# Column-tiled dense products ahead of weighting passes, and a reordered prologue, in a fused attention and gated-MLP kernel

## The chip, the cores and the metric

One core of a Trainium2 chip runs the whole program. The time is device microseconds of one execution. Before the change it is 325.08 us, the median of three runs (324.86 to 325.14). The profile is one further execution of the same program.

In a profile, PE is the matrix engine (TensorE) and PEld its weight loads, DVE is VectorE, ACT ScalarE, POOL GpSimd, SP the engine that issues the DMAs here. A product is one TensorE instruction: a stationary tile (the weights, up to 128 rows by 128 columns) against a moving tile whose columns (up to 512) stream through.

## What is computed

```python
xn = layernorm(x)                              # 2048 rows, 640 columns
q, k, v = xn @ wq, xn @ wk, xn @ wv            # 32 heads of 20 columns, 4 segments of 512 rows
for s in range(4):
    p = softmax(qs @ ks.T * 20**-0.5 + causal mask)      # within the segment
    a_dot = p @ vs
    a_mem = (phi(qs) @ M) / (phi(qs) @ z + 1e-6)         # memory of the segments before
    o = g * a_mem + (1 - g) * a_dot                      # g = sigmoid(beta), per head
    M, z = M + phi(ks).T @ vs, z + sum(phi(ks))          # phi(t) = t + 1 if t > 0 else exp(t)
s = o @ wo
h = (sigmoid(xn @ w_gate) * (xn @ w_up)) @ w_down        # 1536 hidden columns
out = x + s * silu(h)
```

Inputs and output are bf16.

## The kernel before, in words

**Tiling.** The rows are worked in four segments of 512 rows, four tiles of 128 rows each. The 640 columns are five chunks of 128 (DC = 5), and two halves of 320 (HB) where an output has rows on the partitions. Nearly all of the matrix work consists of dense products with a full 128x128 stationary tile and a moving tile of 512 columns (k_chunk, q_chunk, gate, up: lines 322, 354, 463, 475) or of 320 columns (v_tile, down, o_proj: lines 396, 488, 534), accumulated over the chunks in one of four PSUM buffers (dtile). Two smaller ones update and read the memory (m_update, mem_read: lines 422, 442).

**Attention.** Eight groups of four heads are worked in four pairs per segment. The scores of a pair are computed in five units (UNITS, line 42), one unit per slot: a unit issues 8 or 16 products whose stationary tiles have 24 rows, four side by side in the array's row strips (scores, line 556), and ACT then takes the exponential of the whole unit (line 567). A weighting pass (weigh_group, line 605) multiplies the exponentials of one group with V: 28 products in seven rounds of four, each with a 128x32 stationary tile, the four of a round side by side in the array's column strips (line 613). It runs at the start of slot u = 3 for the pair's first group, and at the start of the next pair's slot u = 0 for its second. The very last pair is weighted in another way (weigh, line 578). One further set of products uses column strips, q_bound (line 369), once per segment.

**The order of the work** is written out: all five engines run their instructions in the order in which the program issues them. A planner (lines 718 to 848) goes through 20 slots per segment, 80 in all. Tasks have due times in slots (PLAN, line 61), and the tasks of segment n + 1 (LayerNorm, V, K, Q, phi) and of segment n - 1 (output projection) fall among the slots of segment n. The products of the gated MLP are the filling (bulk): each slot gets a share such that dense work per slot is level, with less where a weighting pass follows (TURN, line 55). In a slot, the order is: weighting pass if there is one, scores, dense work. LAG (line 57) sets how long after a pass its output is transposed by a DMA (LAG[0]) and divided (LAG[1], LAG[2]).

**The prologue** is startup (line 651), with the loads from line 188 on ahead of it. SP issues rows 0, 1 and 2 of x (x_first, 128 rows each), the left half of Wv, rows 3, the right half of Wv, Wk, Wq and the rest. PE first runs 40 dummy products on the identity (warm, line 646). For each 128 rows DVE takes the statistics (ln_stats, line 267), POOL the reciprocal root, DVE normalizes (ln_norm, line 288), PE transposes in five products (line 300), and ACT copies the transposed rows out of PSUM into xnT (line 301). Then come the V products of rows 0 to 2, the five chunks of K and of Q, and the first chunks of the MLP. POOL also fills what has to be constant: the three key tiles KT with ones (lines 653, 671, 674; 128 x 2048 bf16 each), the columns of ones in the V tiles (v_ones), the head indicators (make_ind) and the block diagonal (make_bd).

Of the kernel before, what the change touches and what calls it, by code (L numbers as in the profile page):

```python
# [56 lines left out]
LAG = [0.8, 2.9, 1.7]  # L57
# [4 lines left out]
    dict(glu=[0.3, -0.46],  # L62
         v=[0.1, 0.64, 1.13, 2.21, 2.84, 3.31, 3.7, 5.69],
         k=[6.2, 6.62, 7.76, 8.11, 9.34],
         q=[9.4, 10.58, 11.42, 11.93, 15.22],
         pk=[9.1, 9.21, 10.27, 11.45, 12.74],
         pq=[14.8, 15.82, 16.1, 17.26, 18.26],
         pk0=[-1.0, -0.69, 1.1, 1.4, 2.04],
         bound=16.1,
         upd=[5.8, 9.09],  # L70
         norm=[-2.2, 0.23],
         late=4.2),
    dict(v=[2.5, 3.15, 4.01, 4.25, 4.7, 4.98, 5.8, 6.15],
         k=[6.2, 6.89, 7.97, 8.13, 8.97],
         q=[12.6, 13.11, 13.88, 14.24, 15.01],
         pk=[10.2, 10.65, 10.99, 12.53, 13.51],
         pq=[14.9, 14.96, 16.25, 16.53, 18.03],
         bound=16.5,
         upd=[9.4, 10.15],
         stats=[-2.0, -0.87, -1.23, 0.15],  # L80
         norm=[0.6, 0.88, 1.63, 3.19],
         proj=[5.7, 6.67, 7.51, 8.45, 9.23, 9.75, 10.77, 11.29],
         read=[2.4, 3.01, 3.92, 4.48, 4.72, 5.2, 6.11, 6.62]),
    dict(v=[3.2, 3.6, 4.46, 4.9, 5.46, 6.06, 6.33, 6.88],
         k=[7.6, 8.55, 9.39, 11.57, 12.48],
         q=[12.8, 13.01, 13.89, 14.4, 14.62],
         pq=[14.5, 16.3, 16.56, 17.42, 18.23],
         bound=15.8,
         upd=[9.7, 12.3],
         stats=[-1.9, -1.66, -0.06, 1.16],  # L90
         norm=[-0.4, 0.1, 1.3, 2.5],
         proj=[4.0, 5.18, 5.84, 6.61, 7.43, 8.68, 9.21, 9.37],
         read=[3.1, 3.6, 5.1, 5.4, 6.8, 7.2, 8.1, 8.6]),
    dict(proj=[5.9, 6.42, 7.54, 8.41, 9.04, 9.62, 10.89, 12.0],
         read=[2.0, 3.79, 4.35, 5.57, 5.85, 7.03, 7.64, 8.63]),
# [4 lines left out]
def kernel(  # L100
# [65 lines left out]


# [15 lines left out]
    def load_proj(name, src, c0=0, c1=D):  # L183
        if c0 == 0:
            W[name] = cpool.tile([P, DC, D], BF, name=f"W{name}")
        nc.sync.dma_start(W[name][:, :, c0:c1], src[:, c0:c1].rearrange("(c p) n -> p c n", p=P))
# [29 lines left out]
    nhalf = cpool.tile([P, 2], F32, name="nhalf")  # L216
# [14 lines left out]
    def v_ones(a, b):  # L231
        for i in range(a, b):
            nc.gpsimd.memset(V[i][:, :, DH:VW], 1.0)
            nc.gpsimd.memset(V[i][:, H, 0:DH], 1.0)
# [32 lines left out]
    def ln_stats(n, p, i0=0, i1=2):  # L267
        s = st[n]
        x = s[f"x{p}"]
        if i0 == 0:  # L270
            s[f"mv{p}"] = lnp.tile([P, 2, 2], F32, name="mv")
            s[f"rstd{p}"] = lnp.tile([P, 2], F32, name="rstd")
        mv, rstd = s[f"mv{p}"], s[f"rstd{p}"]
        for i in range(i0, i1):
            bs = lnp.tile([P, 2, 6], F32, name="bs")
            nc.vector.bn_stats(bs[:, 0, :], x[:, i, 0:HB])
            nc.vector.bn_stats(bs[:, 1, :], x[:, i, HB:D])
            nc.vector.bn_aggr(mv[:, i, :], bs[:])

        def root():  # L280
            nc.gpsimd.tensor_scalar(rstd[:, i0:i1], mv[:, i0:i1, 1], EPS, None, op0=ALU.add)
            nc.gpsimd.tensor_tensor(rstd[:, i0:i1], rstd[:, i0:i1], nhalf[:, i0:i1], op=ALU.pow)
        if n <= 1:
            root()
        else:
            later(0.6, root)

    def ln_norm(n, p, i):
        s = st[n]
        if "xnT" not in s:  # L290
            s["xnT"] = xpool.tile([P, DC, L], BF, name="xnT")
        xn = lnp.tile([P, D], BF, name="xn")
        nc.vector.tensor_scalar(xn[:], s[f"x{p}"][:, i, :], s[f"mv{p}"][:, i, 0:1], s[f"rstd{p}"][:, i:i + 1],  # L293
                                op0=ALU.subtract, op1=ALU.mult)
        j = 2 * p + i
        dst = s["xnT"][:, :, j * P:(j + 1) * P]
        if n == 0:
            pT = dtile([P, DC, P], BF, "pT")
            for c in range(DC):
                nc.tensor.transpose(pT[:, c, :], xn[:, c * P:(c + 1) * P], ident[:])  # L300
            nc.scalar.copy(dst, pT[:])
# [20 lines left out]
    def k_chunk(n, c):  # L322
        s = st[n]
        if c == 0:
            s["k5"] = stg.tile([P, DC, L], BF, name="k5")
            s["kabs"] = stg.tile([P, DC], F32, name="kabs")
        ps = dtile([P, L], F32, "psk")
        for k in range(DC):
            nc.tensor.matmul(ps[:], lhsT=W["k"][:, k, c * P:(c + 1) * P], rhs=s["xnT"][:, k, :],  # L329
                             start=(k == 0), stop=(k == DC - 1))  # L330
# [23 lines left out]
    def q_chunk(n, c):  # L354
# [5 lines left out]
        for k in range(DC):  # L360
            nc.tensor.matmul(ps[:], lhsT=W["q"][:, k, c * P:(c + 1) * P], rhs=s["xnT"][:, k, :],  # L361
                             start=(k == 0), stop=(k == DC - 1))
# [33 lines left out]
    def v_tile(n, j, half):  # L396
        s = st[n]
        ps = dtile([P, HB], F32, "psv")
        for k in range(DC):
            nc.tensor.matmul(ps[:], lhsT=s["xnT"][:, k, j * P:(j + 1) * P],  # L400
                             rhs=W["v"][:, k, half * HB:(half + 1) * HB],
                             start=(k == 0), stop=(k == DC - 1))
        va = V[4 * (n % 2) + j]
        evacuate(va[:, half * 16:(half + 1) * 16, 0:DH], ps[:].rearrange("p (h e) -> p h e", e=DH))
# [17 lines left out]
    def m_update(n, cs):  # L422
        s = st[n]
        dm = dtile([P, len(cs), HW * VW], F32, "dm")
        for i, c in enumerate(cs):
            w = (H1[c] - H0[c]) * VW
            for j in range(4):
                nc.tensor.matmul(dm[:, i, 0:w], lhsT=s["pkt"][:, j, c * P:(c + 1) * P],  # L428
                                 rhs=V[4 * (n % 2) + j][:, H0[c]:H1[c], :].rearrange("p h e -> p (h e)"),
                                 start=(j == 0), stop=(j == 3))  # L430
# [11 lines left out]
    def mem_read(n, j, b):  # L442
# [5 lines left out]
        for i, c in enumerate(parts):  # L448
            lo, hi = max(H0[c], 16 * b), min(H1[c], 16 * b + 16)
            nc.tensor.matmul(am[:, lo - 16 * b:hi - 16 * b, :].rearrange("p h e -> p (h e)"),  # L450
                             lhsT=s["q5"][:, c, j * P:(j + 1) * P],
                             rhs=Mbd[:, c, lo - H0[c]:hi - H0[c], :].rearrange("p h e -> p (h e)"),
                             start=(i == 0), stop=True, skip_group_check=True)
# [9 lines left out]
    def gate(n, f):  # L463
# [3 lines left out]
        for k in range(DC):  # L467
            nc.tensor.matmul(gp[:], lhsT=Wg[f // 4][:, k, fo:fo + P], rhs=s["xnT"][:, k, :],  # L468
                             start=(k == 0), stop=(k == DC - 1))
# [5 lines left out]
    def up(n, f):  # L475
# [4 lines left out]
        for k in range(DC):  # L480
            nc.tensor.matmul(ps[:], lhsT=Wu[f // 4][:, k, fo:fo + P], rhs=s["xnT"][:, k, :],  # L481
                             start=(k == 0), stop=(k == DC - 1))
# [5 lines left out]
    def down(n, j, half):  # L488
# [9 lines left out]
        for f in range(FC):  # L498
            nc.tensor.matmul(yp[:], lhsT=s["hT"][f][:, j * P:(j + 1) * P], rhs=W["d"][:, f, hs],  # L499
                             start=(f == 0), stop=(f == FC - 1))  # L500
# [33 lines left out]
    def o_proj(n, j, half):  # L534
# [5 lines left out]
        for c in range(DC):  # L540
            nc.tensor.matmul(sp[:], lhsT=s["oT"][:, j, c, :], rhs=W["o"][:, c, hs],  # L541
                             start=(c == 0), stop=(c == DC - 1))
# [108 lines left out]
    def startup():  # L651
        warm(WARM)
        nc.gpsimd.memset(KT[0][:], 1.0)
# [12 lines left out]
        v_tile(0, 2, 0)  # L666
        v_tile(0, 1, 1)
        v_tile(0, 2, 1)
        v_ones(0, 4)
        make_ind()  # L670
        nc.gpsimd.memset(KT[1][:], 1.0)
        for c in range(DC):
            k_chunk(0, c)
        nc.gpsimd.memset(KT[2][:], 1.0)
        stage_out(0, 0, Ks, KT, "k5")
        for c in range(DC):
# [7 lines left out]
            if c < 2:  # L684
                ln_stats(1, 0, c, c + 1)
# [10 lines left out]
        ln_stats(1, 1, 0, 1)  # L696
        gates()
        take(2)
        ln_stats(1, 1, 1, 2)
# [12 lines left out]
    for i in range(4):  # L712
        at(5.2 + 0.5 * i, 0, load_late, "d", B_w_down, 3 * i, 3 * i + 3)
    for i, (a, b) in enumerate(((0, 3), (3, 5))):
        at(20.3 + 0.6 * i, 0, load_late, "o", A_wo, a, b)


    for n in range(NSEG):
        w, t = NSLOT * n, PLAN[n]
        m = n + 1  # L720
        if m < NSEG:
            if n:
                for i in range(4):
                    at(w + t["stats"][i], 0.1, ln_stats, m, i // 2, i % 2, i % 2 + 1)
# [50 lines left out]
    for n in range(NSEG):  # L775
# [46 lines left out]
        for slot in range(NSLOT):  # L822
# [9 lines left out]
            pts[u] = scores(n, pair, u)  # L832
            delay[0] = True
# [17 lines left out]

    take()
# [41 lines left out]
```

## Time and profile before

| what | us |
|---|---|
| median of three runs | 325.08 |
| the profiled execution | 324.93 |
| its span | 323.2 |
| PE busy | 317.4 |
| ACT, DVE, POOL busy | 241.0, 219.9, 132.3 |
| products on PE (and as many weight loads) | 3426 |
| first real product (psv, line 400) | 7.40 after the span's start |
| first Wk product (psk, line 329) | 12.54 |
| first scores (Sps, line 562) | 32.70 |
| last product | ends 319.5 |

How to read the lines that follow. In a list in order of time, a line gives the start in us from the span's start, the length, the engine, the line of the kernel, the instruction, output <- inputs, the shape, and how many such instructions are merged in it; in brackets stands the idle time of the engine before it and what ended it. For a matrix product "128*32" means 128 rows and 32 columns of weights, and the length contains the time that a result takes through the array, so that the next line starts before the length is over: starts are compared, not ends. In the chain that ended last, a line is the start, the time that this piece adds to the chain, and what it is. PEclk is the clock granted to TensorE, in tenths of full speed, in 40 slices of the span.

### The profile page before, as it was taken

To read this page: it belongs to the slowest core of one execution; us is meant where nothing else is said; L and a number is where in the kernel's file an instruction comes from. 1 tells how busy PE (TensorE), PEld (TensorE's weight loads), DVE (VectorE), ACT (ScalarE), POOL (GpSimd) and SP (SyncE) were. 2 spreads that over 40 slices of the span, in tenths; PEclk is the share of its full clock that TensorE was granted. 3 is DMA by queue.
4 is the path that set the end of the run, shared out by engine and by line. 5 is a ranking of instruction groups with operands and counts; after the bars stand their busy time and mean duration, and the time that the engine had idled before them with its cause. 6 is when DMAs were issued, how large, how long until landed. Compare 5 with 4: busy or idle time off the path is not lost.

```text
span 323.2 us, 8536 instructions
## 1 busy us (share of the span) xinstructions
PE 317.4 (98%) x3426; PEld 172.7 (53%) x3426; DVE 219.9 (68%) x517; ACT 241.0 (75%) x270; POOL 132.3 (41%) x234
## 2 busy tenths in 40 slices
PE   7999999999999999999999999999999999999995
PEld 7544555445564565644556466544456555444773
DVE  5366854797688678698687748875846578544445
ACT  3653897889997776688788787767898987798720
POOL 6727322233346221583306622363515352554303
PEclk9999999999999999999999999999999999999999
DMA  7986996977845561534552274342431272221032
GB/s 220 364 248 170 192 223 167 242 125 174 166 113 113 118 111 52 151 93 96 142 145 55 57 117 113 68 128 59 153 94 34 43 135 75 83 79 19 2 65 83
DMA packets 70968, 39.50 MB, mean 122 GB/s; under 512 B 44944, under 2 KB 70928, under 8 KB 70928
## 3 DMA queue, kind: packets, MB, share of 16 engines
q1 hardware_dynamic: 70928, 38.95, 50.4%
q8 instruction: 27, 0.44, 0.6%
q14 instruction: 13, 0.11, 0.1%
HBM read 20.19 MB, written 8.39 MB: 88 GB/s over the span
## 4 chain that ended last, share of the span: by engine, by line
PE 88%; DVE 6%; DMA 4%; POOL 1%; issue 1%; ACT 0%; DVEq 0%
PE up L481 16%; PE gp L468 16%; PE yp L499 15%; PE Sps L562 8%; PE psk L329 7%; PE AT L613 6%; PE psq L361 6%; PE psv L400 5%; PE sp L541 5%; PE am L450 1%; DMA Qs<-q 1%; DMA xnT<-xn 1%; PE dm L428 1%; DVE xn L293 1%; DMA xt<-in_A_x_dram 1%
## 5 line engine op out<-in xcount | busy, mean ns | idle before, releaser
L567 ACT ACTIVATE pt<-Sps 128x2048 bf16<-128x2048 f32 x80 | 150.5, 1881 | 24.3 <-PE Sps L562 21.9
L571 POOL TENSOR_SCALAR_AFFINE_SELECT pt<-pt 128x512 bf16<-128x512 bf16 x128 | 81.3, 672 | 152.0 <-ACT pt L567 151.9
L481 PE MATMUL up<-xnT,Wu 128*128 128x512 bf16 x240 | 63.0, 380 | 0.0
L468 PE MATMUL gp<-xnT,Wg 128*128 128x512 bf16 x240 | 62.3, 380 | 0.0
L499 PE MATMUL yp<-Wd,hT 128*128 128x320 bf16 x384 | 56.9, 299 | 0.1
L485 DVE SCALAR_TENSOR_TENSOR hT<-hT,up 128x512 bf16<-128x512 bf16 x48 | 32.8, 682 | 28.4 <-PE up L481 19.8
L499 PEld LDWEIGHTS <-hT 128*128 128x128 bf16 x384 | 35.7, 98 | 17.8 <-issue 3.7
L481 PEld LDWEIGHTS <-Wu 128*128 128x128 bf16 x240 | 21.8, 98 | 26.3 <-issue 4.6
L468 PEld LDWEIGHTS <-Wg 128*128 128x128 bf16 x240 | 21.6, 98 | 24.1 <-issue 2.5
L473 ACT ACTIVATE hT<-gp 128x512 bf16<-128x512 f32 x48 | 28.8, 599 | 7.4 <-PE gp L468 7.1
L562 PE MATMUL Sps<-QT,KT 24*128 24x128 bf16 (+2 forms) x896 | 31.9, 241 | 0.0
L617 ACT CAST ats<-AT 128x512 bf16<-128x512 f32 x30 | 17.7, 590 | 15.6 <-PE AT L613 15.1
L505 DVE SCALAR_TENSOR_TENSOR aa<-t,yp 128x320 bf16<-128x320 bf16 x32 | 15.3, 482 | 18.5 <-ACT t L503 18.4
L400 PE MATMUL psv<-Wv,xnT 128*128 128x320 bf16 x160 | 25.5, 299 | 0.3 <-DMA xnT<-xn 0.2
L541 PE MATMUL sp<-Wo,oT 128*128 128x320 bf16 x160 | 25.5, 299 | 0.0
L562 PEld LDWEIGHTS <-KT 24*128 24x128 bf16 x896 | 13.1, 92 | 21.9 <-issue 20.2
L329 PE MATMUL psk<-xnT,Wk 128*128 128x512 bf16 x100 | 24.0, 379 | 0.0
L361 PE MATMUL psq<-xnT,Wq 128*128 128x512 bf16 x100 | 23.6, 379 | 0.0
L613 PE MATMUL AT<-pt,va 128*32 128x128 bf16 (+1 forms) x840 | 22.1, 244 | 0.0
L543 DVE SCALAR_TENSOR_TENSOR aa<-aa,sp 128x320 bf16<-128x320 bf16 x32 | 15.4, 483 | 9.3 <-PE sp L541 9.3
L613 PEld LDWEIGHTS <-va 128*32 128x32 bf16 x840 | 14.4, 97 | 12.0 <-issue 6.2
L503 ACT ACTIVATE t<-yp 128x320 bf16<-128x320 f32 x32 | 14.0, 440 | 7.1 <-PE yp L499 7.1
(81 smaller groups left out, 365.3 us busy)
## 6 DMA issues: line engine op xcount, KB each, us to landing
KT<-Ks SPq DMA_DIRECT2D x32, 80.0 KB
QT<-Qs SPq DMA_DIRECT2D x32, 80.0 KB
xr<-in_A_x_dram SPq DMA_DIRECT2D x15, 160.0 KB
out_dram<-xr SPq DMA_DIRECT2D x15, 160.0 KB
xt<-in_A_x_dram SPq DMA_DIRECT2D x6, 320.0 KB
Wg<-in_B_w_gate_dram SPq DMA_DIRECT2D x3, 640.0 KB
Wu<-in_B_w_up_dram SPq DMA_DIRECT2D x3, 640.0 KB
Wd<-in_B_w_down_dram SPq DMA_DIRECT2D x4, 480.0 KB
```

What stands on the lines that cost most here:

```text
L329: nc.tensor.matmul(ps[:], lhsT=W["k"][:, k, c * P:(c + 1) * P], rhs=s["xnT"][:, k, :], start=(k == 0), stop=(k == DC - 1))
L361: nc.tensor.matmul(ps[:], lhsT=W["q"][:, k, c * P:(c + 1) * P], rhs=s["xnT"][:, k, :], start=(k == 0), stop=(k == DC - 1))
L400: nc.tensor.matmul(ps[:], lhsT=s["xnT"][:, k, j * P:(j + 1) * P], rhs=W["v"][:, k, half * HB:(half + 1) * HB], start=(k == 0), stop=(k == ...
L468: nc.tensor.matmul(gp[:], lhsT=Wg[f // 4][:, k, fo:fo + P], rhs=s["xnT"][:, k, :], start=(k == 0), stop=(k == DC - 1))
L481: nc.tensor.matmul(ps[:], lhsT=Wu[f // 4][:, k, fo:fo + P], rhs=s["xnT"][:, k, :], start=(k == 0), stop=(k == DC - 1))
L485: empty(lambda: nc.vector.scalar_tensor_tensor(out=h[:], in0=h[:], scalar=1.0, in1=ps[:], op0=ALU.add, op1=ALU.mult), own)
L499: nc.tensor.matmul(yp[:], lhsT=s["hT"][f][:, j * P:(j + 1) * P], rhs=W["d"][:, f, hs], start=(f == 0), stop=(f == FC - 1))
L541: nc.tensor.matmul(sp[:], lhsT=s["oT"][:, j, c, :], rhs=W["o"][:, c, hs], start=(c == 0), stop=(c == DC - 1))
L562: nc.tensor.matmul(Sps[:, r, c0:c0 + cnt * P], lhsT=kt[32 * r:32 * r + KR, gi, kb * P:(kb + 1) * P], rhs=qt[32 * r:32 * r + KR, gi, qb * P ...
L567: nc.scalar.activation(pt[:], Sps[:], ACT.Exp, scale=SCALE)
L571: nc.gpsimd.affine_select(out=diag, in_=diag, compare_op=ALU.is_ge, fill=0.0, base=0, pattern=[[0, 4], [1, P]], channel_multiplier=-1)
L613: nc.tensor.matmul(AT[32 * r:32 * r + 32, qb * P:(qb + cnt) * P], lhsT=v[:, h0:h0 + 32], rhs=pts[u][:, r, c0:c0 + cnt * P], start=(i == 0) ...
```

## The change

1. A helper `mm` replaces the plain product in every dense place. With the flag `columns` set it issues four products of 128x32 weights, one per column strip, in place of one of 128x128. The planner sets the flag after the scores of units 2 and 4 (the last pair apart), and clears it after the scores of the others, so that the dense work between those scores and the weighting pass behind them is issued in column strips, the same strips as the pass uses.
2. The prologue: Wv is loaded in five row blocks, four ahead of rows 2 and one ahead of rows 3. VectorE fills all three key tiles and the ones of V tiles 0 and 1, ahead of the first statistics; POOL makes the indicators and the ones of V tiles 2 and 3 before its first root. The first transposed rows are copied in two pieces (two chunks, then three), the transposes of the second rows are issued between the second and third part of the first V product, and the dummy products between them are 4, not 10. The order of statistics, norms and V products differs accordingly.
3. The due times in PLAN and LAG differ, and the loads of w_down and wo get theirs from PLAN.

```diff
-LAG = [0.8, 2.9, 1.7]
+LAG = [0.4, 2.8, 1.7]
...
-    dict(glu=[0.3, -0.46],
-         v=[0.1, 0.64, 1.13, 2.21, 2.84, 3.31, 3.7, 5.69],
...
-         pk0=[-1.0, -0.69, 1.1, 1.4, 2.04],
-         bound=16.1,
-         upd=[5.8, 9.09],
-         norm=[-2.2, 0.23],
-         late=4.2),
+    dict(glu=[2.0, -0.3],
+         wd=[5.1, 5.93, 6.04, 6.47],
+         wo=[19.4, 19.9],
+         v=[0.1, 0.64, 1.44, 2.0, 2.53, 3.0, 3.39, 5.38],
...
+         pk0=[-0.2, 0.53, 1.66, 2.21, 4.03],
+         bound=16.0,
+         upd=[5.6, 9.89],
+         norm=[-0.4, -0.33],
+         late=4.1),
...
+    columns = [False]
+
+    def mm(ps, lhsT, rhs, start, stop):
+        if columns[0]:
+            for b in range(0, P, 32):
+                nc.tensor.matmul(ps[b:b + 32], lhsT=lhsT[:, b:b + 32], rhs=rhs, start=start, stop=stop,
+                                 tile_position=(0, b), skip_group_check=True)
+        else:
+            nc.tensor.matmul(ps, lhsT=lhsT, rhs=rhs, start=start, stop=stop, skip_group_check=True)
...
-    for j in range(3):
-        x_first(j)
-    load_proj("v", A_wv, 0, HB)
+    W["v"] = cpool.tile([P, DC, D], BF, name="Wv")
+
+    def load_v(a, b):
+        for c in range(a, b):
+            nc.sync.dma_start(W["v"][:, c, :], A_wv[c * P:(c + 1) * P, :])
+
+    x_first(0)
+    x_first(1)
+    load_v(0, 4)
+    x_first(2)
+    load_v(4, DC)
     x_first(3)
-    load_proj("v", A_wv, HB, D)
     load_proj("k", A_wk)
...
-            nc.scalar.copy(dst, pT[:])
+            for a, b in ((0, 2), (2, DC)) if j == 0 else ((0, DC),):
+                nc.scalar.copy(dst[:, a:b], pT[:, a:b])
...
-    def v_tile(n, j, half):
+    def v_tile(n, j, half, between=None):
         s = st[n]
         ps = dtile([P, HB], F32, "psv")
         for k in range(DC):
-            nc.tensor.matmul(ps[:], lhsT=s["xnT"][:, k, j * P:(j + 1) * P],
-                             rhs=W["v"][:, k, half * HB:(half + 1) * HB],
-                             start=(k == 0), stop=(k == DC - 1))
+            mm(ps[:], s["xnT"][:, k, j * P:(j + 1) * P], W["v"][:, k, half * HB:(half + 1) * HB],
+               k == 0, k == DC - 1)
+            if k == 1 and between:
+                between()
...
         warm(WARM)
-        nc.gpsimd.memset(KT[0][:], 1.0)
-        ln_stats(0, 0, 0, 1)
-        ln_stats(0, 0, 1, 2)
+        for t in KT:
+            nc.vector.memset(t[:], 1.0)
+        v_ones(0, 2, nc.vector)
+        make_ind()
+        v_ones(2, 4)
+        ln_stats(0, 0, 0)
+        ln_stats(0, 0, 1)
         ln_norm(0, 0, 0)
-        warm(10)
-        ln_stats(0, 1, 0, 1)
-        ln_norm(0, 0, 1)
-        v_tile(0, 0, 0)
-        ln_stats(0, 1, 1, 2)
+        warm(4)
+        v_tile(0, 0, 0, lambda: ln_norm(0, 0, 1))
+        v_tile(0, 0, 1)
+        ln_stats(0, 1, 0)
         v_tile(0, 1, 0)
+        ln_stats(0, 1, 1)
         ln_norm(0, 1, 0)
-        v_tile(0, 0, 1)
+        v_tile(0, 1, 1)
         ln_norm(0, 1, 1)
         v_tile(0, 2, 0)
-        v_tile(0, 1, 1)
         v_tile(0, 2, 1)
-        v_ones(0, 4)
-        make_ind()
-        nc.gpsimd.memset(KT[1][:], 1.0)
         for c in range(DC):
             k_chunk(0, c)
-        nc.gpsimd.memset(KT[2][:], 1.0)
...
             pts[u] = scores(n, pair, u)
+            columns[0] = u in (2, NU - 1) and not old(n, pair)
             delay[0] = True
...
+    columns[0] = False
     take()
```

The other dense places (k_chunk, q_chunk, m_update, mem_read, gate, up, down, o_proj) call `mm` in the same way, with the same operands as before. The due times of the other three segments differ by up to 2.4 slots and mostly by less than 0.6.

More of the change, by code (lines that the diff above doesn't have):

```diff
@@ L84 @@
[L84 to L95, printed above, removed]
+    dict(glu=[2.0, -0.3],
+         wd=[5.1, 5.93, 6.04, 6.47],
+         wo=[19.4, 19.9],
+         v=[0.1, 0.64, 1.44, 2.0, 2.53, 3.0, 3.39, 5.38],
+         k=[6.0, 7.32, 7.56, 8.11, 8.84],
+         q=[9.9, 10.58, 11.52, 12.03, 15.32],
+         pk=[9.4, 9.72, 10.99, 11.98, 13.4],
+         pq=[14.2, 15.42, 16.0, 17.16, 18.16],
+         pk0=[-0.2, 0.53, 1.66, 2.21, 4.03],
[3 more added lines that the diff above has]
+         late=4.1),
@@ new lines @@
+    dict(v=[2.5, 3.15, 4.01, 4.25, 4.7, 4.98, 5.8, 6.15],
+         k=[6.5, 6.84, 7.85, 8.2, 8.8],
+         q=[12.6, 13.31, 13.49, 14.7, 15.0],
+         pk=[10.2, 10.65, 10.99, 12.43, 13.71],
+         pq=[14.4, 14.47, 15.88, 16.49, 18.11],
+         bound=16.4,
+         upd=[9.2, 10.33],
+         stats=[-1.3, -0.67, -1.63, -0.35],
+         norm=[0.4, 0.88, 2.73, 3.59],
+         proj=[5.6, 6.57, 7.41, 8.35, 9.13, 9.65, 10.77, 11.19],
+         read=[1.9, 3.31, 3.92, 4.28, 4.92, 5.2, 6.11, 6.62]),
@@ new lines @@
+    dict(v=[3.2, 3.64, 4.59, 4.85, 5.69, 6.24, 6.64, 7.03],
+         k=[7.5, 8.29, 9.81, 10.62, 11.67],
+         q=[12.0, 12.71, 13.39, 13.8, 14.01],
+         pq=[13.9, 16.51, 16.69, 17.49, 18.23],
+         bound=15.2,
+         upd=[9.8, 11.83],
+         stats=[-1.7, -0.93, 0.71, 3.56],
+         norm=[0.4, 0.84, 2.77, 4.39],
+         proj=[4.2, 4.88, 6.04, 6.81, 7.63, 8.88, 9.41, 9.57],
+         read=[3.1, 3.6, 5.1, 5.3, 6.7, 7.2, 7.6, 8.4]),
+    dict(proj=[5.3, 6.52, 7.34, 8.01, 9.34, 9.92, 11.49, 12.2],
+         read=[2.0, 3.19, 4.95, 5.87, 6.95, 7.33, 8.34, 8.63]),
@@ L229, with v_ones @@
     Mbd = cpool.tile([P, DC, HW, VW], BF, name="Mbd")
-    def v_ones(a, b):
+    def v_ones(a, b, eng=nc.gpsimd):
         for i in range(a, b):
-            nc.gpsimd.memset(V[i][:, :, DH:VW], 1.0)
-            nc.gpsimd.memset(V[i][:, H, 0:DH], 1.0)
+            eng.memset(V[i][:, :, DH:VW], 1.0)
+            eng.memset(V[i][:, H, 0:DH], 1.0)
     def make_ind():
@@ L360, in q_chunk @@
         for k in range(DC):
-            nc.tensor.matmul(ps[:], lhsT=W["q"][:, k, c * P:(c + 1) * P], rhs=s["xnT"][:, k, :],
-                             start=(k == 0), stop=(k == DC - 1))
+            mm(ps[:], W["q"][:, k, c * P:(c + 1) * P], s["xnT"][:, k, :], k == 0, k == DC - 1)
         (nc.vector.tensor_copy if n else nc.scalar.copy)(s["q5"][:, c, :], ps[:])
@@ L467, in gate @@
         for k in range(DC):
-            nc.tensor.matmul(gp[:], lhsT=Wg[f // 4][:, k, fo:fo + P], rhs=s["xnT"][:, k, :],
-                             start=(k == 0), stop=(k == DC - 1))
+            mm(gp[:], Wg[f // 4][:, k, fo:fo + P], s["xnT"][:, k, :], k == 0, k == DC - 1)
             yield
@@ L480, in up @@
         for k in range(DC):
-            nc.tensor.matmul(ps[:], lhsT=Wu[f // 4][:, k, fo:fo + P], rhs=s["xnT"][:, k, :],
-                             start=(k == 0), stop=(k == DC - 1))
+            mm(ps[:], Wu[f // 4][:, k, fo:fo + P], s["xnT"][:, k, :], k == 0, k == DC - 1)
             yield
```

74 lines of the change are left out of this document (26 added, 48 removed).

## The prediction

> **What bounds the kernel now.** I read the page first, then the chain that ended last, then the PE's work in order of time, then all engines in the first 16 us.
>
> Busy time, the granted clock and the chain by engine:
>
> ```profile
> PE 317.4 (98%) x3426; PEld 172.7 (53%) x3426; DVE 219.9 (68%) x517; ACT 241.0 (75%) x270; POOL 132.3 (41%) x234
> PEclk9999999999999999999999999999999999999999
> PE 88%; DVE 6%; DMA 4%; POOL 1%; issue 1%; ACT 0%; DVEq 0%
> ```
>
> PE is the bound nearly everywhere, so a microsecond that PE loses or gains is one of the span. Two lines of the chain give the price of a dense product:
>
> ```profile
> 10.67 2.04 PE psv L400 x15
> 18.10 5.40 PE psq L361 x25
> ```
>
> A 320-column product is 2.04/15 = 0.136 us, a 512-column one 5.40/25 = 0.216. Next PE in order of time, around two weighting passes (line 613, 128x32 weights), the scores (line 562, 24 rows) and the bound (line 374):
>
> ```profile
> 78.37 2.35 PE L499 MATMUL yp<-Wd,hT 128*128 128x320 bf16 x16
> 80.64 0.73 PE L613 MATMUL AT<-pt,va 128*32 128x256 bf16 x28
> 81.31 0.40 PE L562 MATMUL Sps<-QT,KT 24*128 24x128 bf16 x16
> 81.65 0.85 PE L499 MATMUL yp<-Wd,hT 128*128 128x320 bf16 x5
> ...
> 85.57 0.60 PE L374 MATMUL cps<-aq,IK 128*32 128x512 bf16 x5
> 86.11 1.53 PE L499 MATMUL yp<-Wd,hT 128*128 128x320 bf16 x10
> ```
>
> Read starts, not lengths. From 78.37 to 80.64 are 2.27 us for 16 products worth 2.18: 0.09 goes where the array passes from full tiles to column tiles. Over all 34 such places the last product is followed after 0.309 (512 columns) or 0.229 (320) instead of 0.216 or 0.136: 0.093 each. The other kinds of passage cost the same 0.09 to 0.10. The pass itself, 28 products in seven rounds of four, streams 1280 columns per column tile: 1280/512 x 0.216 = 0.54 of its 0.67 us, the rest being the next passage. So four column tiles run side by side at the dense rate, weights included.
>
> Last, the prologue, all engines:
>
> ```profile
> 1.34 1.81 POOL L653 MEMSET KT<- 128x2048 bf16 x1
> 1.45 4.45 PE L649 MATMUL wps<-ident 128*128 128x128 bf16 x40 [1.45 <-POOL ident L220]
> 3.12 0.49 DVE L276 BATCH_NORM_STATS2 bs<-xt 128x6 f32<-128x320 bf16 x1 [3.12 <-DMA xt<-in_A_x_dram]
> 5.26 0.45 DVE L293 TENSOR_SCALAR xn<-xt,mv,rstd 128x640 bf16<-128x640 bf16 x1
> 5.77 0.60 PE L300 MATMUL pT<-ident,xn 128*128 128x128 bf16 x5
> 6.40 0.69 ACT L301 COPY xnT<-pT 128x640 bf16<-128x640 bf16 x1 [4.33 <-PE pT L300]
> 7.40 1.80 PE L400 MATMUL psv<-Wv,xnT 128*128 128x320 bf16 x10
> 12.54 3.83 PE L329 MATMUL psk<-xnT,Wk 128*128 128x512 bf16 x17
> 14.44 0.69 DVE L341 TENSOR_REDUCE kabs<-k 128x1 f32<-128x512 bf16 x1 [4.28 <-ACT k L320]
> 21.08 0.24 DVE L364 TENSOR_SCALAR aq<-q 128x512 uint16<-128x512 uint16 x1
> ```
>
> PE's first real product (7.40) hangs on a chain: rows land (3.12), DVE statistics, POOL root, DVE norm (5.26), transposes, ACT copy. DVE is free until 3.12 and not longer. From 12.54 to 32.7 PE runs without a gap, so whatever delays 12.54 delays the end.
>
> **The change, part by part.** The sum is made against the profiled execution: 324.93 us, a span of 323.2 and 1.7 around it; 0.15 below the median of 325.08.
>
> *Column tiles.* Every dense product between the scores of units 2 and 4 and the weighting pass behind them (all but the last pair) is issued as four 128x32 products. There are 30 such stretches, with 473 of the 1670 full products counted in order of time. The passage full to column ahead of 30 passes goes: 30 x 0.093 = 2.8 us gained. The scores are then followed by column instead of full tiles, one passage either way. PE gains 3 x 473, about 1420 products and as many weight loads. The pass shows eight such instructions per 0.056 us (128 columns) and line 585's weighting at the end runs 40 pairs in 1.00 us, 0.10 for four; a dense round lasts 0.136 or 0.216, so they fit. What would end late is PE's instruction stream, for which see C.
>
> *VectorE fills the key tiles.* Three fills of 128x2048 bf16 and four small ones of V now stand on DVE's queue ahead of the first statistics; behind them wait every norm, so the transposes, ACT's copies and all of PE. On POOL these fills cost nothing: the first lay before 4.34, where POOL waited for DVE anyway, the others beside PE work. No DVE fill is in this trace. Low end: the 16-bit pass over 512 elements, 0.24 us, four times as long but for a fixed part of about 0.1 (32 elements take 0.14): 0.66. High end: from 320 elements in 0.48 to 512 in 0.69 is 1.1 ns an element, so 0.69 + 1536 x 0.0011 = 2.3. POOL's own fill of this tile is 1.81. I take 2.1, between the row that is the same operation on the same tile and the DVE rows that go an element at a time; a fill has no input to pack. The Trainium skill, "VectorE: DVE Perf Modes", section "Zero memsets can be issued as uint32 (trn2)", says that a memset takes one cycle per element whatever the type; by that 2048 elements are an estimated 2.13 us, by the 16-bit row 0.66, and no run here shows which.
>
> DVE starts with the other engines at 0.78: 0.78 + 3 x 2.1 + 0.4 for the small fills = 7.5 against 3.12, so the first statistics come 4.35 late. The first norm moves from 5.26 to 9.6, transposes to 10.1, copy to 10.75.
>
> *First copy in two pieces.* 640 columns take 0.69, 320 take 0.43, so 256 about 0.38: the first product can start at 11.15 (with pT of the second rows now behind two of its five parts), against 7.40: 3.75 late.
>
> *From there to Wk.* DVE: second norm 10.75 to 11.15, statistics of rows 2 and 3 to 13.3, their roots 0.9 each, norms at 13.3 and 14.3. PE: six V products of 0.68 and three transposes of 0.28, waiting 0.3 for the third rows; the Wk products start at 16.5 against 12.54: 3.95 late.
>
> *Clock.* The 40 dummy products take 0.107 each, the later transposes 0.056: the array ran at half speed until about 5.5. They still end at 5.9, and now 4.2 us of idleness follow. No such gap is in this trace. If the clock holds: nothing. If it falls and takes the same 4 us to rise, the two transposes and three V products up to 14.3 take twice as long, 2.6, less the 0.3 of waiting and what the norms allow: about 2. I take 1.2, the middle. The Trainium skill, "TensorE: Matmul & The Clock Gate", section "What's actually happening", has one idle window of about 3.4 us halve the clock; by it the sum would lie at the upper half of this term.
>
> *Wv in row blocks, fewer dummies.* SP issues five loads for two, 0.45 each; rows 2 go from third to seventh in its queue, 1.71 to 3.5, rows 3 from 2.65 to 4.4, Wk from 3.69 to 4.9. The first rows took 2.3 to land; 5.8 and 6.7 are well before 11.15, when DVE asks now, and before 6.85, when it would ask with fast fills. Wk is wanted at 16.5. Nothing.
>
> *Plan and lag.* Stalls above 0.1 us in the main loop are two: 0.35 at 40.0 (a transposed xn) and 0.28 at 164.5. Earlier norms may free them; a transpose of ats issued 0.4 of a 3.4 us slot sooner can hold what SP has queued behind it (relays of K and Q). Between -0.6 and +0.7; I take nothing. Wg's last third, 1.7 slots later, then issued near 47.7, still lands some 7 us ahead of its use at 57.3.
>
> Sum: 324.93 - 2.8 + 3.95 + 1.2 = 327.3.
>
> **The rivals.**
> A, the forecast: slow fills on the path. 325.5 (clock holds, main loop gains) to 328.9 (all terms high). For it: a fill reads nothing, and no one-pass DVE row writes 2048 elements in under 0.8. Against: the 0.24 row.
> B, ends the other way: a fill on DVE runs like the 16-bit row, 0.66. Then fills and V's end at 0.78 + 2.0 + 0.4 = 3.2, when the rows land; the split copy brings Wk 0.3 forward: 324.93 - 2.8 - 0.3 = 321.8. It decides from 1.7 us a fill downward: there the prologue loses 2.8 (statistics 3.2 late, less 0.4), all that the column tiles bring.
> B2, in between (1.0 to 1.7 a fill, or column tiles that save more): 322.2 to 325.5.
> C: PE's instructions can't be supplied at 59 per us over a stretch of dense 320-column products (8 per 0.136). If each of 473 rounds took 0.02 more, 9.5 us: above 330. The 40 pairs in 1.00 us speak against it.
>
> **How the numbers follow.** A 0.69, B 0.16, B2 0.11, C 0.04. The forecast is A's: 327.3, A's own range 325.5 to 328.9. To leave out no more than 2 in 10 the range reaches down through B2 to B: 321.6 to 328.9. A difference of 0.2%, 0.65 us, is about what a measurement of this kernel tells from none. Slower: A 0.66 and C 0.04, 0.70. Within: 0.03 of A and 0.03 of B2, 0.06. Faster: B and 0.08 of B2, 0.24.
>
> **What would show it.** DVE fills of KT of about 2 us each from 0.8 on, and the first statistics at 7.5, waiting for DVE's own queue and not for the rows; psv at 11 to 12, psk at 16.5 to 18; PE's spacing in the first V products 0.136 or 0.267. In the loop: PE with about 4840 products, last dense round to pass at 0.216 or 0.136 with no 0.09 between. I am wrong if the fills are over by 3.2, or if a dense round in column tiles is longer than 0.216 and 0.136.

## The result, and the profile after

The changed kernel takes 328.95 us (median of six runs, 328.46 to 332.08) against 325.15 before (324.86 to 325.37): 1.0139 times as long over all runs, 95% interval 1.0111 to 1.0167 (the two medians alone give 1.0117). It is slower, as forecast, but by 3.8 us instead of 2.2, and it ends 0.05 above the range. The profiled execution took 329.85 us, 0.9 above its median; its span is 328.1 against 323.2.

Two lines of the page, busy time and granted clock:

```profile
PE 316.3 (96%) x4812; PEld 179.9 (55%) x4812; DVE 226.5 (69%) x525; ACT 241.1 (73%) x270; POOL 126.0 (38%) x227
PEclk9599999999999999999999999999999999999999
```

PE issues 1386 more products (about 1420 forecast), and the clock has a hole in the second slice, 8.2 to 16.4 us. All engines, in order of time, in the prologue:

```profile
1.28 1.76 DVE L664 MEMSET KT<- 128x2048 bf16 x1 [1.28 <-PEq L889]
3.42 1.76 DVE L664 MEMSET KT<- 128x2048 bf16 x1 [0.38 <-issue]
5.56 1.76 DVE L664 MEMSET KT<- 128x2048 bf16 x1 [0.38 <-issue]
...
7.43 0.43 DVE L293 BATCH_NORM_STATS2 bs<-xt 128x6 f32<-128x320 bf16 x1
...
9.50 0.45 DVE L310 TENSOR_SCALAR xn<-xt,mv,rstd 128x640 bf16<-128x640 bf16 x1
...
11.19 0.71 PE L177 MATMUL psv<-Wv,xnT 128*128 128x320 bf16 x2
...
12.23 3.38 PE L177 MATMUL psv<-Wv,xnT 128*128 128x320 bf16 x13
...
18.09 4.26 PE L177 MATMUL psk<-xnT,Wk 128*128 128x512 bf16 x19
```

The fills start every 2.14 us (a row's length, 1.76, is not what it costs), and the first statistics come at 7.43, 4.3 late, with no wait for the rows. The 13 V products from 12.23 run at half speed: they are spaced 0.267 until about 15.2. The Wk products start at 18.09 instead of 12.54.

In the main loop, PE in order of time shows column tiles at work, 15 rounds of four from 84.40, then the pass:

```profile
84.08 0.40 PE L572 MATMUL Sps<-QT,KT 24*128 24x384 bf16 x8
84.40 2.22 PE L174 MATMUL yp<-Wd,hT 128*32 128x320 bf16 x60
86.45 0.72 PE L623 MATMUL AT<-pt,va 128*32 128x256 bf16 x28
```

The 15 rounds take 2.05, 0.137 each, and there is no gap before the pass. But all engines, in order of time, around 47 and 125 show two waits that the kernel before does not have (the number in brackets is the idle time by the profile; by the start-to-start rule given below they are 1.22 and 0.91):

```profile
47.08 0.86 PE L174 MATMUL psv<-Wv,xnT 128*32 128x320 bf16 x20 [1.06 <-DMA xnT<-xn]
...
125.41 0.85 PE L177 MATMUL psv<-Wv,xnT 128*128 128x320 bf16 x5 [0.74 <-DMA xnT<-xn]
```

To compare whole traces I split each span in three: up to the first scores; PE's waits after that (a product that starts more than 0.13 us after the one before has streamed through, 0.095 for a passage between tilings taken off); and the rest. In us, by the profiled executions, with the median time of all runs of the kernel beside them:

| kernel | first Wk product | first scores | waits of PE | rest | median |
|---|---|---|---|---|---|
| before | 12.54 | 32.71 | 0.63 | 289.9 | 325.15 |
| changed | 18.09 | 38.25 | 2.48 | 287.4 | 328.95 |
| e1 fills on POOL | 13.89 | 34.05 | 1.25 | 287.3 | 325.66 |
| e2 no column tiles | 18.10 | 38.26 | 4.79 | 290.2 | 334.55 |
| e3 old PLAN and LAG | 18.56 | 38.72 | 1.13 | 287.3 | 328.92 |
| e4 115 dummy products | 16.48 | 36.85 | 4.09 | 287.7 | 329.65 |
| e5 fills on POOL, rows first | 13.13 | 33.29 | 2.40 | 287.5 | 324.81 |
| e6 before + column tiles | 12.60 | 32.76 | 4.04 | 286.9 | 324.89 |
| e7 32-bit fills | 13.28 | 33.45 | 1.78 | 287.2 | 325.31 |
| e8 e6 + new PLAN, LAG | 12.93 | 33.10 | 2.28 | 287.0 | 324.08 |
| e9 e6 + two norms earlier | 12.57 | 32.73 | 4.85 | 287.1 | 325.29 |
| e10 before + new PLAN, LAG | 12.51 | 32.67 | 3.27 | 289.9 | 327.53 |
| e11 fills behind the norms | 15.11 | 35.60 | 1.45 | 287.3 | 325.71 |
| e12 e8 + norms earlier | 12.70 | 32.87 | 5.62 | 287.0 | 326.72 |

From before to changed: 5.55 to the first scores, 1.85 more waiting, 2.5 less of the rest, together 4.9, the difference of the spans. The kernel before took 325.06 to 325.5 in the later comparisons; ratios are to the kernel before on the same chip. One of e12's twelve runs, 330.13, counts as slow and is left out of its median and its ratio.

### The profile page after: what moved, and what is told of

It reads as the page before. It is cut to its first block, busy times and chain, and to the rows that moved or that the text cites. A ratio compares the mean times of both kernels' runs of the same rounds, so it can differ in the third digit from the quotient of the medians.

```text
span 328.1 us, 11321 instructions
## 1 busy us (share of the span) xinstructions
PE 316.3 (96%) x4812; PEld 179.9 (55%) x4812; DVE 226.5 (69%) x525; ACT 241.1 (73%) x270; POOL 126.0 (38%) x227
## 4 chain that ended last, share of the span: by engine, by line
PE 91%; DVE 4%; DMA 3%; issue 1%; POOL 0%; ACT 0%; DVEq 0%; POOLq 0%
PE gp L177 12%; PE up L177 12%; PE yp L177 11%; PE Sps L572 8%; PE yp L174 5%; PE psk L177 5%; PE AT L623 5%; PE up L174 5%; PE psv L177 5%; PE psq L177 4%; PE gp L174 4%; PE sp L174 3%; DMA xnT<-xn 3%; PE sp L177 2%; PE psq L174 2%; PE psk L174 2%
## 5 line engine op out<-in xcount | busy, mean ns | idle before, releaser
L177 PE MATMUL gp<-xnT,Wg 128*128 128x512 bf16 x191 | 49.1, 380 | 0.0
L177 PE MATMUL up<-xnT,Wu 128*128 128x512 bf16 x170 | 44.7, 380 | 0.0
L177 PE MATMUL yp<-Wd,hT 128*128 128x320 bf16 x262 | 38.8, 300 | 0.0
L177 PEld LDWEIGHTS <-hT 128*128 128x128 bf16 x262 | 24.3, 98 | 11.8 <-issue 1.9
L177 PEld LDWEIGHTS <-Wg 128*128 128x128 bf16 x191 | 17.6, 98 | 19.7 <-issue 1.3
L177 PEld LDWEIGHTS <-Wu 128*128 128x128 bf16 x170 | 15.7, 98 | 17.7 <-issue 1.5
L177 PE MATMUL psv<-Wv,xnT 128*128 128x320 bf16 x110 | 19.3, 320 | 0.8 <-DMA xnT<-xn 0.7
L514 ACT ACTIVATE t<-yp 128x320 bf16<-128x320 f32 x32 | 13.9, 438 | 7.0 <-PE yp L177 6.0
L610 DVE TENSOR_TENSOR od<-Asb,rd 128x320 bf16<-128x320 bf16 x30 | 18.1, 603 | 1.0
L174 PE MATMUL up<-xnT,Wu 128*32 128x512 bf16 x280 | 18.3, 381 | 0.0
L523 POOL TENSOR_TENSOR od<-od,om 128x320 bf16<-128x320 bf16 x20 | 17.1, 869 | 2.6 <-DVE od L610 2.6
```

The source lines that it names most:

```text
L174: nc.tensor.matmul(ps[b:b + 32], lhsT=lhsT[:, b:b + 32], rhs=rhs, start=start, stop=stop, tile_position=(0, b), skip_group_check=True)
L177: nc.tensor.matmul(ps, lhsT=lhsT, rhs=rhs, start=start, stop=stop, skip_group_check=True)
L523: eng.tensor_tensor(o, o, st[n]["om"][:, :, cs], op=ALU.add)
L610: nc.vector.tensor_tensor(s["od"][:, :, 4 * g * DH:(4 * g + 4) * DH].rearrange("p q (r e) -> p q r e", e=DH), A[:, :, :, 0:DH], rd[:].unsq ...
```

## Experiments

**e1. The fills back on POOL.**

```diff
-        for t in KT:
-            nc.vector.memset(t[:], 1.0)
-        v_ones(0, 2, nc.vector)
-        make_ind()
-        v_ones(2, 4)
+        nc.gpsimd.memset(KT[0][:], 1.0)
...
         v_tile(0, 2, 1)
+        v_ones(0, 4)
+        make_ind()
+        nc.gpsimd.memset(KT[1][:], 1.0)
```

(KT[2] follows the K chunks, as before.)

> The changed kernel with its fills back on POOL, where the kernel before has them; all else as changed. Theory 1 (the fills hold VectorE's queue ahead of the first statistics, and the array's clock falls meanwhile): first statistics at 3.1 us when the rows land, first Wk product at about 12.2 to 12.5 instead of 18.1, time 323.1 to 323.5. Rival (the loss lies in the order of the loads, or in the column tiles): first statistics at 3.1 all the same, but rows 2 or Wv come late and the Wk products start after 14, or they start at 12.5 and the time stays above 326.

Measured: 325.66 us, ratio 1.0011 (0.9986 to 1.0036). Most of the loss is the fills: 3.3 of the 3.8 us are gone. But the Wk products come at 13.89, not 12.2. DVE in order of time:

```profile
3.06 0.49 DVE L293 BATCH_NORM_STATS2 bs<-xt 128x6 f32<-128x320 bf16 x1 [3.06 <-DMA xt<-in_A_x_dram]
...
7.20 0.50 DVE L293 BATCH_NORM_STATS2 bs<-xt 128x6 f32<-128x320 bf16 x1 [0.39 <-DMA xt<-in_A_x_dram]
...
8.99 0.49 DVE L293 BATCH_NORM_STATS2 bs<-xt 128x6 f32<-128x320 bf16 x1 [0.66 <-DMA xt<-in_A_x_dram]
```

Rows 2 (issued 3.60) are waited for until 7.2, rows 3 (issued 4.54) until 9.0. The rival was right about the loads: their order has a price of its own, which the slow fills covered. The time lies between theory 1's 323.5 and the rival's 326.

**e2. No column tiles.**

```diff
-            columns[0] = u in (2, NU - 1) and not old(n, pair)
+            columns[0] = False
```

> The changed kernel with the flag for column tiles never set, so every dense product is a full one. Theory 1 (each of 30 passages from full to column tiles costs 0.093, and a dense round in column tiles costs what a full product does): 2.5 to 2.8 us longer than the changed kernel, about 331.6. Rival (the column tiles cost PE time, by weight loads or instructions): shorter than the changed kernel, under 328.5.

Measured: 334.55, ratio 1.0258 (1.0220 to 1.0297), 5.6 above the changed kernel and 3 above theory 1's 331.6. The rest grows by 2.8, as theory 1 has it; 2.3 more of waiting come on top, which no theory had. Column tiles do not cost PE time, and under the new due times they are worth more than the passages they save.

**e3. The old PLAN and LAG** in the changed kernel (the constants of the kernel before, nothing else).

> The changed kernel with PLAN and LAG of the kernel before. Theory 1 (the two waits of PE for a transposed xn, 1.22 us at 47.1 and 0.91 at 125.4, come from the new due times): both gone, the waits of before of 0.3 in their place, 1.2 to 1.9 us shorter than the changed kernel, 327.0 to 327.7. Rival (they come from the late prologue or from the column tiles): the waits stay and the time is within 0.4 of the changed kernel.

Measured: 328.92, ratio 1.0112 (1.0089 to 1.0134). The waits at 47.1 and 125.4 fall to 0.28 and nothing, and the sum from 2.48 to 1.13, but the median does not move (328.95 before the edit). In its profile the half speed lasted longer: the 13 V products took 3.67 and not 3.38, and Wk came at 18.56. So theory 1 was wrong about the time. About the waits it fits this trace, but one trace does not show that the due times make them: e4 below has the new due times, and there the first of the two is 0.28 as well.

**e4. A longer run of dummy products.**

```diff
-WARM = 40
+WARM = 115
```

> The changed kernel with 115 dummy products at the start instead of 40, so that PE works until about 9.9 us and not until 5.6. Theory 1 (after 4.4 us of idleness the array runs at half speed again until about 15): the V products are spaced 0.136 instead of 0.267, the first Wk product starts at about 16.5 instead of 18.1, time 1.4 to 1.6 us shorter than the changed kernel, about 327.4. Rival (the clock falls for another reason than idleness, or VectorE's chain sets the Wk products anyway): the Wk products start at 17.8 or later and the time is within 0.4 of the changed kernel.

Measured: the Wk products start at 16.48. PE in order of time, where the same 13 V products take 1.93 and not 3.38:

```profile
11.49 1.93 PE L177 MATMUL psv<-Wv,xnT 128*128 128x320 bf16 x13
...
16.48 0.81 PE L177 MATMUL psk<-xnT,Wk 128*128 128x512 bf16 x3
```

At the first Wk product the clock term is 1.61 us, and it comes from the idle stretch. Yet the time is 329.65 (1.0128, 1.0106 to 1.0149), no shorter: PE waits 1.6 more in the main loop, 1.83 of it at one place, where a K product needs a PSUM buffer that VectorE, held by a transpose of keys (pkt), has not emptied. All engines, in order of time, at this place in e4:

```profile
60.29 0.40 PE L572 MATMUL Sps<-QT,KT 24*128 24x256 bf16 x8
...
63.24 0.69 DVE L336 CAST k<-psk 128x512 bf16<-128x512 f32 x1 [3.92 <-DMA pkt<-k]
...
63.98 1.26 PE L174 MATMUL psk<-xnT,Wk 128*32 128x512 bf16 x20 [1.67 <-DVE k L336]
...
65.06 0.74 PE L623 MATMUL AT<-pt,va 128*32 128x128 bf16 x28
```

and in the changed kernel:

```profile
61.85 0.40 PE L572 MATMUL Sps<-QT,KT 24*128 24x256 bf16 x8
...
63.02 0.69 DVE L336 CAST k<-psk 128x512 bf16<-128x512 f32 x1 [2.15 <-DMA pkt<-k]
...
64.84 0.74 PE L623 MATMUL AT<-pt,va 128*32 128x128 bf16 x28
```

At these scores PE in e4 is 1.56 us ahead. VectorE's copy of the keys starts no sooner, since the transpose that it waits for lands no sooner, and at the weighting pass the lead is gone. This was the first sign that time which PE gains need not reach the end.

**e5. Rows ahead of Wv**, with the fills on POOL as in e1. Beside e1's edit:

```diff
     x_first(1)
-    load_v(0, 4)
     x_first(2)
-    load_v(4, DC)
+    load_v(0, 3)
     x_first(3)
+    load_v(3, DC)
```

> The changed kernel with its fills back on POOL (as in e1) and rows 0, 1, 2 loaded ahead of Wv, rows 3 behind three of its five row blocks. Theory 2 (with the fills out of the way it is the order of the loads that holds the prologue: in e1 the statistics of rows 2 wait for their landing until 7.2 and those of rows 3 until 9.0): no such waits, first Wk product at 12.0 to 12.4 instead of 13.9, time 1.5 us shorter than e1, 323.8 to 324.3. Rival (POOL's roots or the new order of the V products hold it): first Wk product still after 13.3, time as e1's 325.7.

Measured: 324.81, ratio 0.9983 (0.9964 to 1.0001); the Wk products at 13.13, between theory and rival, like the time. The waits for rows are gone, but the first V product, a sum of five parts, now stops ahead of its fifth part for Wv's last block (PE in order of time):

```profile
7.16 0.65 PE L177 MATMUL psv<-Wv,xnT 128*128 128x320 bf16 x2
8.99 0.70 PE L177 MATMUL psv<-Wv,xnT 128*128 128x320 bf16 x4 [1.18 <-DMA Wv<-in_A_wv_dram]
```

With row blocks the first V product needs all five blocks, 800 KB; with the column half of the kernel before it needs 400 KB. Here, what is loaded first delays the other.

**e6. Column tiles alone**: the helper `mm`, the flag, and nothing else of the change.

> The kernel before with the column tiles alone; prologue, PLAN and LAG as before. Theory 1: 30 passages fewer, 2.7 us shorter than before, 322.2 to 322.7, with PE's waits in the main loop near before's 0.6. Rival (what PE gains it waits for elsewhere, since the main loop's transfers and VectorE do not come sooner): waits above 2 us, time above 323.8.

Measured: 324.89, ratio 0.9996 (0.9987 to 1.0005). The rest falls by 3.0, and the waits rise by 3.4. The rival, in full. Two waits make up most. All engines, in order of time, around 120 in e6:

```profile
115.72 1.21 SPq L315 DMA_TRANSPOSE xnT<-xn  x1
...
120.13 0.85 PE L175 MATMUL psv<-Wv,xnT 128*128 128x320 bf16 x5 [1.51 <-DMA xnT<-xn]
```

and in the kernel before, where the transpose goes out 2 us sooner and the product finds it ready:

```profile
113.71 1.90 SPq L305 DMA_TRANSPOSE xnT<-xn  x1
...
118.57 0.84 PE L400 MATMUL psv<-Wv,xnT 128*128 128x320 bf16 x5
```

The other, DVE and PE in order of time in e6: VectorE stands at phi, which overwrites q in place while a DMA still reads it, and PE has no free PSUM buffer until VectorE comes round to emptying one.

```profile
163.62 0.29 DVE L420 TENSOR_SCALAR q<-q 128x512 bf16<-128x512 bf16 x1 [3.31 <-DMA Qs<-q]
...
166.38 0.88 DVE L506 SCALAR_TENSOR_TENSOR aa<-t,yp 128x320 bf16<-128x320 bf16 x2
...
166.92 1.81 PE L172 MATMUL yp<-Wd,hT 128*32 128x320 bf16 x48 [1.00 <-DVE aa L506]
```

**e7. The same fills in 32-bit words.**

```diff
-            nc.vector.memset(t[:], 1.0)
+            nc.vector.memset(t[:].rearrange("p a b -> p (a b)").bitcast(U32), 0x3F803F80)
```

> The changed kernel with the three key tiles filled as 1024 elements of 32 bits, 0x3F803F80, on VectorE at the same place. Theory 1 (a fill takes VectorE one cycle per element whatever its width, 2.14 us from start to start for 2048): 1.07 from start to start, first statistics at about 4.7 instead of 7.4; PE is idle for 1.8 us and not 4.4, so the clock holds, and the first Wk product starts at 13.8 to 14.2 instead of 18.1; time about 325 to 326. Rival 1 (time goes by bytes): spaced 2.14, nothing changes. Rival 2 (the clock falls after the shorter gap too): V products spaced 0.267, first Wk product at about 15.4.

Measured: 325.31, ratio 1.0009 (0.9997 to 1.0021). DVE in order of time:

```profile
1.07 0.91 DVE L665 MEMSET KT<- 128x1024 uint32 x1 [1.07 <-PEq L890]
2.14 0.91 DVE L665 MEMSET KT<- 128x1024 uint32 x1 [0.16 <-issue]
3.22 0.91 DVE L665 MEMSET KT<- 128x1024 uint32 x1 [0.16 <-issue]
...
4.23 0.43 DVE L294 BATCH_NORM_STATS2 bs<-xt 128x6 f32<-128x320 bf16 x1
```

Half the elements, half the time, for the same bytes. The first statistics come 3.2 sooner than in the changed kernel, and they and the Wk products (13.28) half a microsecond sooner than expected. The V products are spaced 0.136 (the clock holds over 0.9 of idleness). One line takes 3.6 us off the changed kernel's median.

**e8. Column tiles and the new PLAN and LAG, prologue as before.**

> The kernel before with the column tiles and with the changed kernel's PLAN and LAG; the prologue as before. Theory 1 as I now have it (the new due times bring PE waits of 1 to 2 us for transposed rows): 323.2 to 324.5. Rival (the waits belong to the late prologue, the due times fit the column tiles): 322.5 or less, waits under 0.6.

Measured: 324.08, ratio 0.9972 (0.9951 to 0.9993): shorter than both kernels, 2.28 of waits. The time is within theory 1's span. Its reason is not what this trace shows: the two longest waits, 1.0 and 0.6 us, are for VectorE, and none above 0.25 is for transposed rows.

**e9. e6 with one transpose's place moved.**

```diff
-         norm=[0.6, 0.88, 1.63, 3.19],
+         norm=[0.6, 0.88, 1.4, 2.5],
```

> e6 (before plus column tiles) with one line of PLAN changed: the last two norms of segment 2's rows (the list of PLAN[1]) are due at 1.4 and 2.5 slots instead of 1.63 and 3.19, so that the transposes of these rows come earlier in SP's queue. Theory 3 (PE gets ahead of transfers whose place in SP's queue did not move; in e6 the V product at 120.1 waits 1.67 us for a transposed xn issued at 115.7): that wait is under 0.3, the others stay, time 1.0 to 1.6 us shorter than e6, 323.3 to 323.9. Rival (the transposes land late whatever their place, because the DMA engines or the transposes' own length hold them): the wait stays above 1 us and the time is as e6's.

Measured: 325.29, ratio 0.9998 (0.9979 to 1.0018). The wait itself went, as theory 3 has it: in e9 the product follows its predecessor (PE in order of time).

```profile
119.27 0.84 PE L175 MATMUL sp<-Wo,oT 128*128 128x320 bf16 x5
119.95 0.84 PE L175 MATMUL psv<-Wv,xnT 128*128 128x320 bf16 x5
```

But the time stayed, and the expected 1.0 to 1.6 us was a miss. In this trace (326.51, 1.2 above the median) there are other waits, 1.37 at 74.8 and 0.93 at 125.0, both for VectorE, and the one at 167 is still there. The one at 74.8 is not a consequence of the edit: until about 105 us every engine runs the same instructions in the same order as in e6. That the one at 125.0 is a consequence is not shown.

**e10. The new PLAN and LAG alone** in the kernel before.

> The kernel before with the changed kernel's PLAN and LAG alone: no column tiles, prologue as before. Theory 3 (these due times move work so that a faster PE finds it ready; with full tiles they have no virtue): within 0.8 of before or longer, 325 to 327, and the waits of PE in the main loop between 0.6 and 3 us. Rival (the new due times are better in themselves): 324.3 or less.

Measured: 327.53, ratio 1.0064 (1.0044 to 1.0084), a little over theory 3's range in the time as in the waits, which are 3.27. The rival fell.

**e11. The fills on VectorE, behind the norm of rows 3.**

```diff
-        for t in KT:
-            nc.vector.memset(t[:], 1.0)
-        v_ones(0, 2, nc.vector)
-        make_ind()
-        v_ones(2, 4)
...
         ln_norm(0, 1, 1)
+        for t in KT:
+            nc.vector.memset(t[:], 1.0)
+        v_ones(0, 4)
+        make_ind()
         v_tile(0, 2, 0)
```

> The changed kernel with the three fills still on VectorE, but behind the norm of rows 3 instead of ahead of the first statistics (V's ones and the indicators on POOL at the same place). Theory 1 (what costs is the place in VectorE's queue, not the engine): first statistics at 3.1, first Wk product as in e1, 13.7 to 14.1, time as e1's, 324.5 to 326. The maxima of K come some 3 us later and delay nothing. Rival (fills on VectorE cost wherever they are, since the K chunks' maxima and the bound wait for them): over 327.

Measured: 325.71, ratio 1.0032 (0.9996 to 1.0068). The time is e1's: the place counts, not the engine. (Three of the ten runs take 327.6 to 329.7; in these the mean granted clock was 0.995, in the others 0.998 or more.) Wk comes at 15.1 rather than 13.9, since in this execution rows 3 landed only at 10.2 (9.0 in e1).

**e12. e8 with norms of two segments sooner** (the values stand in the expectation).

> e8 (before, column tiles, the new PLAN and LAG) with the norms of the last rows of segments 2 and 3 due 0.6 to 0.8 slots sooner (2.0 and 2.9 for 2.73 and 3.59; 2.2 and 3.6 for 2.77 and 4.39, the last statistics at 2.6 for 3.56). Theory 3: waits for transposed rows in segments 1 and 2 go where a run has them, time 0.2 to 0.8 shorter than e8's 324.1. Rival (in e8 the other waits, of VectorE for the transposed outputs of a weighting pass, hold it): no difference from e8, or longer, since VectorE's queue gets the norms sooner.

Measured: 326.72, ratio 1.0035 (1.0005 to 1.0065) against e8's 0.9972, so about 2 us longer, with 5.62 of waits. A miss. Waits for transposed rows did not go (1.3 and 0.4), and the two others above 1 us (1.5 and 1.3) are for VectorE. The time fits the rival's second half; its reason, that VectorE gets the norms sooner, is not shown.

## Why the prediction was right or wrong

**The step that failed: waits put at nothing.** The forecast counts a microsecond that PE loses or gains as one of the span (the sentence under its first lines), and it puts PE's waits in the main loop at nothing, -0.6 to +0.7 at most (*Plan and lag*). The profiled execution has 1.85 us more of waits than the kernel before. This took the sum out of its range: 324.93 + 5.55 - 2.5 + 1.85 = 329.8, against 324.93 + 5.15 - 2.8 = 327.3; the prologue is 0.4 above its terms and the column tiles are 0.3 short of theirs. Only this execution was split, so how the median's 3.8 us divide is not known. The range was also added up short: "all terms high", with fills of 2.3 in place of 2.1, is 324.93 - 2.8 + 3.95 + 0.6 + 2.0 + 0.7 = 329.4 and not 328.9.

**The fills: right.** 2.1 us each was taken from rows that bound them at 0.66 and 2.3; they measure 2.14 from start to start. Their rows end at 3.04, 5.18 and 7.32; counted back at 2.14 each, the first began at an estimated 0.90 (0.78 was taken). The four small ones cost next to nothing, where 0.4 was taken. The first statistics came at 7.43 (7.5 forecast), the first V product at 11.19 (11.15). Rival B fell: e7, where half the elements take half the time for the same bytes, shows that a fill goes by the element, so the 16-bit row behind B's 0.66 does not carry over to it. The Trainium skill, "VectorE: DVE Perf Modes", section "Zero memsets can be issued as uint32 (trn2)", states one cycle per element whatever the type; 2.14 for 2048 and 1.07 for 1024 agree, and with a constant that is not zero.

**The Wk products: right but for the clock.** Without the clock's fall 16.5 was forecast, and e4 without the fall has 16.48. The clock term was taken at 1.2, the middle of 0 to 2; at the Wk products it measures 1.61. The Trainium skill, "TensorE: Matmul & The Clock Gate", section "What's actually happening", has an idle window of about 3.4 us halve the clock. The traces agree roughly: PE stood from 5.5 to 10.0, and the granted clock was 1.00 until 8.3 and 0.50 from 8.4 to 15.1, so it fell some 3 us into the gap; after e7's 0.9 it held. (At the start of the kernel before, half speed lasted until about 6.1 and not 5.5: the first transposes are spaced 0.106 up to there.)

In the time of the whole kernel this term does not show. Two of the six runs of the changed kernel have a mean granted clock of 1.00, so no such fall, and they take 328.46 and 332.08, the shortest and the longest; the four with 0.987 to 0.995 take 328.71 to 329.85. In e4 it was 0.998 or more in all four runs, and they take 329.21 to 330.32.

**Column tiles: right as PE time, wrong as time.** 2.8 us fewer of passages were forecast, and dense rounds at the full rate; the rest falls by 2.5 to 3.0 in all pairs of traces, and rival C fell (0.137 a round, and 0.216 for 512 columns). What failed is that this gain was booked as time of the kernel. PE was busy for 98%, but in e6 a transpose and VectorE's emptying of a PSUM buffer, which PE had waited for by 0.3 us at most in the kernel before, came 1.5 and 1.0 us too late: e6 gives back all that it gains.

**Plan and lag: mis-sized.** Two stalls of before were listed and nothing taken for new ones. What the due times do can be read only together with the tiles. Ratio to the kernel before, its prologue kept:

| | old PLAN, LAG | new PLAN, LAG |
|---|---|---|
| full tiles | 1 | 1.0064 (e10) |
| column tiles | 0.9996 (e6) | 0.9972 (e8) |

Each part alone brings nothing or a loss; together they bring 0.9 us (0.2 to 1.6 by the interval), a third of what PE saves. So the tiles are worth nothing under the old due times and about 3 us under the new ones, and in the changed kernel 5.6 (e2): they are not what made it slower. That the new due times are worth something only to a PE that comes sooner fits these four ratios. With the changed prologue they bring nothing even so: 1.0112 with the old ones (e3), 1.0139 with the new.

A list of the single waits of one trace could not have shown that. In e9 the wait that was aimed at went and the time stayed. And the waits differ without an edit to the main loop: from the first scores on, the changed kernel, e1, e4, e5, e7 and e8 run the same instructions in the same order on every engine, and their traces have between 1.25 and 4.09 of waits. What decides which transfers come late in one of them stays open.

**Order of the loads: right here, wrong in its reason.** "Nothing" holds in the changed kernel, whose statistics ask for rows 2 at 11.0. But the landings of 5.8 and 6.7 were worked out with the 2.3 us that the first rows took with nothing ahead of them. In e1 they land at 7.2 and 9.0. The time of rival B (321.8) was too low for that reason as well: e1, whose fills cost VectorE nothing, has its Wk products at 13.89 and takes 325.66.

What stays open: why the profiled run of the changed kernel is 0.9 above its median, and which of VectorE's queue, SP's queue and the transfers themselves would have to be relieved for PE's whole gain of 2.5 to 3.0 us to arrive. Phi writing to a second buffer, which should take away the second wait shown in e6, was not tried.

## What to carry to other kernels

An engine that is busy for 98% of the span sets a least time, and no more: time taken from it is a gain only as far as the engines and transfers that supply it have slack, and that slack is to be tested before the gain is booked; the list of waits in one trace does not show it. Work that is free on an idle engine is paid in full when it is put ahead of the first instruction of a chain, however idle that engine looks later; ask what each queue does first. A schedule written out by hand belongs to the durations it was written for, so test a faster part together with due times moved for it, and the due times alone as well.

## What the runs showed that I had not expected

- A fill's row in the trace is shorter than its cost: 1.76 us long, 2.14 from start to start (0.91 and 1.07 for half the elements).
- The same load lands later with more issued ahead of it: 160 KB of rows land 2.3 us after issue with nothing ahead, 3.6 with six loads of 160 KB ahead (e1), and 4.5 to 5.7 with eight (e1, e11).
- Some kernels spread more from run to run than the kernel before (324.9 to 325.4 in the first comparison, up to 327.5 in the later ones): e8 with both column tiles and new due times from 322.2 to 326.6, e12 from 324.3 to 329.0. With one of the two alone they do not: e6 324.3 to 325.8, e10 326.9 to 328.2. In e1, e5 and e11 the longest runs are those in which the granted clock fell, to a mean of 0.992 to 0.995.
